# Inner products in place of halves for twelve of tile 1's outer products, with GpSimd summing and storing earlier

## The chip, the cores and the metric

The kernel runs on one core of one Trainium2 chip. The metric is the device time of one execution in microseconds (us). Before the change it is 1041.65 us, the median of three runs (1039.41 to 1042.3).

The engines are named as in the profile: PE is TensorE's matrix multiply, PEld its weight load, DVE is VectorE, ACT is ScalarE, POOL is GpSimd and SP is SyncE. A name such as ACTq is the sequencer of an engine, which also issues DMAs.

## The reference

Two blocks in a row, all in f32. First a retention layer, then a gated feed-forward layer on its output:

```
ret = (q k^T / sqrt(64)) * decay(head, row, column)     # 8 batches, 8 heads, 576 positions, 64 wide
x   = ret v, heads side by side                         # 4608 tokens x 512
g   = x @ w_gate ; h = g * sigmoid(g) * (x @ w_val)     # 4608 x 1536
out = h @ w_out                                         # 4608 x 512
```

## The kernel before

**Tiles.** The 4608 tokens are cut into tile 0 (512 tokens) and tiles 1 to 4 (1024 tokens each). Each tile has an up stage (`x @ w_gate`, `x @ w_val`) and a down stage (`h @ w_out`). The retention of later tokens is cut into ticks, whose small 64 x 64 multiplies are put between those of the stages. Tile 0 is computed plainly (`up0`, `down0`, `out0`). Tiles 1 to 4 use fast matrix multiplication, in which sums of blocks replace some multiplies.

**The up stage (`up_stage`, line 1114).** The 1536 hidden columns are cut into three quarters `qd`, each with its gate and value weights. In a quarter there are seven outer products, taken in the order `SETS = (1, 2, 6, 7, 4, 5, 3)`, one for each set of operand blocks. On the weight side, sets 1, 2, 7 and 3 are blocks of the weights as loaded, and sets 5, 6, 7 and 4 are made by outer sums (`outer_sums` in `w_sets`, two instructions of 128 x 512 each; 7 in place). The activation side has its own outer sums (`outer_sums` in `x_sets`).

An outer product is a 2 x 2 block product and is done in one of two ways:

- Plain (`PLAIN`, line 110): eight slots, two for each of its four corners. The accumulator holds a corner, which is read once or twice (`whole_read`).
- As seven inner products: seven slots. They need further, smaller sums on both sides (`inner_sums`, four sums of 128 x 256 on the activation side and four on the weight side for each set), and their banks are read in part (`first_read`), then again (`second_read`), because corners are put together from several products. The slots are numbered 1 to 7 as in `PLACE`. Slots 7 and 4 of an outer product are done among the slots of the next one.

A slot (`multiply`) is two f32 multiplies of a 128 x 128 weight block with 128 x 256 activations into one PSUM bank, four records of PE in the profile. Four banks, bankA, bankB, bankC and bankE, go round (`free`, `taken`).

Before the change all 21 outer products of tile 1 are plain, and all those of tiles 2 to 4 are inner. Tile 1 (`busy` in the code) also prepares the weights for the others: POOL makes the outer and inner sums of all 21 weight sets, and ACT's queue stores them to DRAM (`up_sets`), raw blocks in two DMAs of 256 KB and the four sums in one of 512 KB. Tiles 2 to 4 fetch them again (`fetch`, ACT's queue).

**Who does what in an up stage.** Sums from banks are DVE's (`combine`, line 1040, is the line that most of them carry), some reads are split into an ACT copy and a POOL sum. When a corner is complete, `finish` has ACT compute silu (line 1177) and, in tile 1, DVE multiply (line 1178); in tiles 2 to 4 POOL multiplies.

**The order.** Nothing is scheduled automatically: the order of the program is the order on each engine's queue. `later(at, ...)` puts work at slot `at`; `go` issues it. A down stage has 26 steps (`down_step`, line 1331) of 12 PE records each; its last five or nine steps also issue the first activation sums of the next tile (`x_first`, line 1079), two at a time, all on POOL. `down0` runs twelve steps of tile 0 in `down_order`. Between them POOL and DVE make the sums of `w_out` (`out_sums`, line 886). `out0` copies the four banks into `hid0[0]`, `[1]`, `[4]` and `[5]` and SP stores them. Those places are where sets 6, 4 and 5 of quarter 0 go next.

Of the kernel before, what the change touches and what calls it, by code (L numbers as in the profile page):

```python
# [109 lines left out]
PLAIN = {(1, qd, o) for qd in range(3) for o in SETS}  # L110
# [21 lines left out]
def kernel(  # L132
# [727 lines left out]
    down_order = [8, 9, 10, 0, 1, 11, 2, 3, 4, 5, 6, 7]  # L860
# [6 lines left out]
    def out0():  # L867
        for i, (bank, o) in enumerate(zip(banks, (hid0[f] for f in (0, 1, 4, 5)), strict=True)):
            nc.scalar.copy(out=o, in_=bank)
            nc.sync.dma_start(out=out[i * P : (i + 1) * P, :], in_=o)  # L870
# [17 lines left out]
    up_sets = [[dr.tile([P, 2048], F32, name=f"up{qd}_{o}") for o in SETS] for qd in range(NQ)]  # L888
# [91 lines left out]
    TURN = {1: [5, 6, 7, 0, 1, 2, 3, 4], 2: [7, 0, 1, 2, 3, 4, 5, 6], 3: [7, 3, 4, 5, 6, 0, 1, 2], 4: [7, 5, 6, 0, 1, 2, 3, 4]}  # L980
# [8 lines left out]
    def fetch_one():  # L989
        what, a, i, lo, width = fetches[fetched[0]]  # L990
        dst = operands[:, lo : lo + width]
        fetched[0] += 1
        if what == "dn":
            queue = nc.sync if a + 1 == NTILE and i >= 8 or a == 1 and i >= 5 else nc.scalar
            queue.dma_start(out=dst, in_=dn_ops[i])
            return
        src = up_sets[a][SETS.index(i)].rearrange("p (g x) -> p g x", g=2)
        nc.scalar.dma_start(out=dst.rearrange("p (g x) -> p g x", g=2), in_=src[:, :, P : 1024])
# [47 lines left out]
    def x_sets(n):  # L1046
# [8 lines left out]
        new = {o: spots[3 * m : 3 * m + 3] for m, o in enumerate((1, 2, 7, 4, 5, 3, 6))}  # L1055
# [23 lines left out]
    def x_first(n):  # L1079

        x_outer, x_inner, *_ = x_sets(n)
        p = nc.gpsimd
        first = x_inner(1, p) + x_outer(5, p) + x_outer(6, p)
        return first + x_outer(3, p) + x_inner(2, p) + x_outer(7, p) if n + 1 == NTILE else first

    def w_sets(qd):
# [3 lines left out]
        new = [rest[:, a : a + 1024].rearrange("p (g j x) -> p g j x", g=2, j=4) for a in (x0_at + 1024, sum_at)]  # L1090
        queue = nc.scalar
        order = (6, 4, 5, 7, 1, 2, 3)
# [5 lines left out]
        def inner_sums(o):  # L1098
            z = lambda k, m: sets[o][:, :, m, k * P : (k + 1) * P]
            to = lambda j: new[order.index(o) % 2][:, :, j]  # L1100
# [5 lines left out]
        def store(o, new_ones):  # L1106
            dst = up_sets[qd][SETS.index(o)].rearrange("p (g x) -> p g x", g=2)
            if new_ones:
                return [lambda: queue.dma_start(out=dst[:, :, 512:1024], in_=new[order.index(o) % 2].rearrange("p g j x -> p g (j x)"))]
            return [lambda m=m: queue.dma_start(out=dst[:, :, TB * (1 - m) : TB * (2 - m)], in_=sets[o][:, :, m]) for m in range(2)]  # L1110

        return sets, order, outer_sums, inner_sums, store

    def up_stage(n):
# [13 lines left out]
        number = {2: 0, 4: 1, 5: 0, 3: 1}  # L1128
# [15 lines left out]
        def to(k, c):  # L1144
            o = seq[k][1]
            return held[c] if o in (1, 6) else kept(k, c) if o == 7 else ends[number[o]][c]
# [4 lines left out]
        def weights_of(k):  # L1151
            qd, o = seq[k]
            if busy:
                sets = w_sets(qd)[0]
                spot = [(kk, m) for m in (1, 0) for kk in range(2)]
                return lambda at: sets[o][:, :, spot[at][1], spot[at][0] * P : (spot[at][0] + 1) * P]
            _, _, _, lo, width = fetches[base + k]
            w = operands[:, lo : lo + width].rearrange("p (g i x) -> p g i x", g=2, x=P)
            return lambda at: w[:, :, at if plain[k] else at - 1]
# [20 lines left out]
        def made(k, c, at):  # L1180
            if seq[k][1] in final:
                waiting.append((at + 3, k, c))

        def whole_read(k, c, bank, at):
            o = seq[k][1]
            if o == 1:
# [8 lines left out]
        def first_read(k, c, bank):  # L1195
            qd, o = seq[k]
            dst = to(k, c)
            if o == 1:
                nc.scalar.copy(out=dst, in_=bank)
            elif o == 5 and c != 12:  # L1200
# [6 lines left out]
            elif qd > 0 and o != 3 and c != 12:  # L1207
                t = ends[0 if o == 4 else 1][c]
# [64 lines left out]
        if not busy:  # L1273
            begin = lambda k: begins[k]
            if n + 1 < NTILE:
                for i, f in enumerate(x_outer(3, nc.vector)):
                    later(i, f)
                for i, f in enumerate(x_inner(2, nc.gpsimd)):
                    later(1 + i, f)
                for i, f in enumerate(x_outer(7, nc.vector)):  # L1280
                    later(3 + 2 * i, f)
# [4 lines left out]
        else:  # L1286
            for i, f in enumerate(x_outer(5, nc.vector) + x_outer(6, nc.vector) + x_outer(7, nc.vector) + x_outer(3, nc.vector)):
                later(i if i < 4 else 2 * i + 2, f)
            for qd in range(NQ):
                at = begins[len(SETS) * qd]  # L1290
                _, order, w_outer, w_inner, store = w_sets(qd)
                for i, f in enumerate([f for o in (5, 6, 7, 4) for f in w_outer(o)]):
                    later(at + i, f)
                for i, o in enumerate(order):
                    for j, f in enumerate(w_inner(o)):
                        later(at + 8 + (13 * i + 3 * j) // 2, f)
                    later(at + 8 + (13 * i + 9) // 2 + 6, *store(o, True))
                for i, o in enumerate((1, 2, 6, 7, 4, 5, 3)):
                    for j, f in enumerate(store(o, False)):
                        later(at + 3 + 5 * i + 2 * j, f)  # L1300

        def go(at):
# [9 lines left out]
            if busy and at in (120, 124, 128):  # L1312
# [15 lines left out]

    firsts = []

    def down_step(n, i):
# [37 lines left out]
        begins = N - 5 if n + 2 < NTILE else N - 9  # L1369
        if i == begins and n + 1 < NTILE:  # L1370
            firsts.extend(x_first(n + 1))
        if i >= begins:
            for f in [firsts.pop(0) for _ in range(min(2, len(firsts)))]:
                f()

# [66 lines left out]
    for m, f in enumerate(down_order):  # L1442
# [7 lines left out]
        if groups:  # L1450
            groups.pop(0)[1]()
    out0()
# [60 lines left out]
```

## Time and profile before

| what | value |
|---|---|
| median of 3 runs | 1041.65 us (1039.41 to 1042.3) |
| profiled execution, its own time | 1044.91 us |
| its span, first to last instruction | 1043.2 us |
| mean granted TensorE clock | 0.997 |
| PE / PEld busy | 98% / 80% |
| DVE / POOL / ACT busy | 66% / 53% / 28% |
| tile 0's down stage (line 864) | 123.6 to 176.6 us |
| tile 1's up stage (line 1163) | 176.6 to 338.0 us |
| tile 1's down stage (line 1342) | 338.0 to 418.0 us |
| up stages of tiles 2, 3 and 4 begin | 418, 638 and 844 us |

How to read it: a row of the timeline is a run of like instructions on one engine, with its start, its length, the engine, the line, the operation, what it writes and reads, the shape and the count; the brackets hold the idle time before it and what ended that. A PE row of eight records is two slots; its length includes the modelled end of the last record, so the pace is read from the starts of successive rows. A view by stretches gives the busy time and the count of instructions of each engine between two times.

### The profile page before, as it was taken

Reading aid. Unit: us, or ns where it says so; the run is one execution under the profiler, and the core shown is the slowest. Engines: PE = TensorE matmul, PEld = TensorE weight load, DVE = VectorE, ACT = ScalarE, POOL = GpSimd, SP = SyncE. Lnnn points to the kernel's source line nnn. Section 1 sums busy time; section 2 is a strip of 40 time slices with the busy share of each in tenths; the row PEclk is TensorE's granted clock in tenths of the full one; section 3 lists DMA queues with packets and bytes.
Section 4 is the critical chain, followed back from the end, with each engine's and each line's share of the span. In section 5 each row is a group of like instructions: output and inputs, shape, how many; then the busy total and the mean of one; then the engine's idle time right before and its main releaser. Section 6 shows DMA issues by size and latency. Waiting matters only on the chain. (4 is left out here: it accounts for less than half of the span.)

```text
span 1043.2 us, 21372 instructions
## 1 busy us (share of the span) xinstructions
PE 1018.3 (98%) x8380; PEld 834.0 (80%) x8380; DVE 692.1 (66%) x1182; ACT 288.2 (28%) x638; POOL 551.0 (53%) x586
## 2 busy tenths in 40 slices
PE   6999999999999999999999999999999999999998
PEld 5655555888788888878888887888888888888887
DVE  4488883675857855875768777857576448566744
ACT  4466532131332321123332111133230012333110
POOL 3402263884635206854657237775582497566615
PEclk9999999999999999999999999999999999999999
DMA  9999887679485886756558767544454444445552
GB/s 241 253 273 240 213 226 252 204 190 253 134 244 156 224 240 198 198 170 172 177 157 242 202 169 203 168 148 142 142 190 152 154 157 150 169 141 176 185 159 96
DMA packets 292364, 197.13 MB, mean 189 GB/s; under 512 B 212968, under 2 KB 251112, under 8 KB 292264
## 3 DMA queue, kind: packets, MB, share of 16 engines
q10 hardware_dynamic: 58960, 121.12, 35.3%
q1 hardware_dynamic: 232664, 74.25, 29.9%
q8 instruction: 66, 1.08, 0.4%
q0 software_dynamic: 640, 0.39, 0.2%
q14 instruction: 34, 0.28, 0.1%
HBM read 154.04 MB, written 41.68 MB: 188 GB/s over the span
## 5 line engine op out<-in xcount | busy, mean ns | idle before, releaser
L1041 POOL TENSOR_TENSOR rest<-rest 128x512 f32<-128x512 f32 (+1 forms) x147 | 155.6, 1073 | 158.6 <-DVE rest L1041 118.9
L1178 POOL TENSOR_TENSOR arena<-rest,io 128x256 f32<-128x256 f32 x144 | 105.4, 744 | 70.8 <-ACT io L1177 70.4
L1177 ACT ACTIVATE io<-rest 128x256 f32<-128x256 f32 x192 | 79.4, 417 | 225.1 <-DVE rest L1041 121.4
L1041 DVE TENSOR_TENSOR rest<-bankA,rest 128x512 f32<-128x512 f32 x100 | 67.7, 686 | 63.2 <-PE bankA L1163 46.2
L1163 PE MATMUL bankE<-rest,arena 128*128 128x256 f32 x424 | 108.0, 380 | 1.3 <-DVE rest L1041 1.2
L1163 PE MATMUL bankB<-rest,arena 128*128 128x256 f32 x416 | 106.4, 381 | 0.2
L1163 PE MATMUL bankA<-rest,arena 128*128 128x256 f32 x392 | 99.9, 381 | 1.4 <-DVE rest L1041 1.2
L1041 DVE TENSOR_TENSOR rest<-bankE,rest 128x512 f32<-128x512 f32 x108 | 73.0, 685 | 41.4 <-PE bankE L1163 23.8
L1041 DVE TENSOR_TENSOR rest<-bankC,rest 128x512 f32<-128x512 f32 x100 | 67.8, 685 | 44.0 <-PE bankC L1163 22.5
L1163 PE MATMUL bankC<-rest,arena 128*128 128x256 f32 x372 | 94.7, 381 | 0.6 <-DVE rest L1041 0.5
L1041 DVE TENSOR_TENSOR rest<-bankB,rest 128x512 f32<-128x512 f32 x101 | 68.7, 686 | 38.2 <-PE bankB L1163 25.0
L1163 PEld LDWEIGHTS bankE<-rest,arena 128*128 128x128 f32 x424 | 79.9, 190 | 14.1 <-DVE rest L1041 2.2
L1163 PEld LDWEIGHTS bankB<-rest,arena 128*128 128x128 f32 x416 | 78.2, 190 | 12.3 <-DVE rest L1041 1.1
L1163 PEld LDWEIGHTS bankA<-rest,arena 128*128 128x128 f32 x392 | 73.8, 190 | 13.6 <-DVE rest L1041 1.8
L1163 PEld LDWEIGHTS bankC<-rest,arena 128*128 128x128 f32 x372 | 69.8, 190 | 12.0 <-DVE rest L1041 2.5
L886 POOL TENSOR_TENSOR rest<-rest 128x256 f32<-128x256 f32 x43 | 35.4, 845 | 67.0 <-DVE rest L407 35.4
L1342 PE MATMUL bankE<-arena 128*128 128x256 f32 x264 | 61.0, 381 | 0.0
L1342 PE MATMUL bankC<-arena 128*128 128x256 f32 x264 | 60.8, 380 | 0.0
L1041 POOL TENSOR_TENSOR rest<-arena 128x256 f32<-128x256 f32 x42 | 31.5, 770 | 51.5 <-DMA up<-rest 51.5
L1342 PE MATMUL bankA<-arena 128*128 128x256 f32 x240 | 55.4, 380 | 1.8 <-POOL arena L886 1.8
L1342 PEld LDWEIGHTS bankC<-arena 128*128 128x128 f32 x264 | 50.0, 190 | 6.9
L1342 PEld LDWEIGHTS bankE<-arena 128*128 128x128 f32 x264 | 49.8, 190 | 6.9
(255 smaller groups left out, 1948.0 us busy)
## 6 DMA issues: line engine op xcount, KB each, us to landing
arena<-up ACTq DMA_DIRECT2D x63, 896.0 KB, 5.0
arena<-dn ACTq DMA_DIRECT2D x65, 384.0 KB, 4.4
arena<-dn SPq DMA_DIRECT2D x39, 384.0 KB, 3.6
up<-arena ACTq DMA_DIRECT2D x42, 256.0 KB, 4.5
up<-rest ACTq DMA_DIRECT2D x21, 512.0 KB, 3.3
dn<-rest SPq DMA_DIRECT2D x78, 128.0 KB, 1.8
out_dram<-rest SPq DMA_DIRECT2D x31, 256.0 KB, 2.6
qk<-in_q_dram SPq DMA_DIRECT2D x108, 72.0 KB, 3.2
```

The source lines that it names most:

```text
L886: eng.tensor_tensor(out=dst, in0=srcs[0], in1=srcs[1], op=ALU.add if op[0] == "add" else ALU.subtract)
L1041: eng.tensor_tensor(out=out, in0=a, in1=b, op=ALU.add if sign > 0 else ALU.subtract)
L1163: m = nc.tensor.matmul(b[:, g * TB : (g + 1) * TB], w[:, g], x, start=(opens and g == 0), stop=True, skip_group_check=True)
L1177: nc.scalar.activation(out=s, in_=src[:, 0:TB], func=AF.Silu)
L1178: (nc.vector if busy else nc.gpsimd).tensor_tensor(out=hid[:, qd, 2 * H + h, 2 * T + t], in0=src[:, TB : 2 * TB], in1=s, op=ALU.mult)
L1342: nc.tensor.matmul(b[:, m * TB : (m + 1) * TB], lhs[:, qd, ts(m, P)], w[:, qd], start=(opens and qd == 0 and m == 0), stop=(qd == NQ - 1), ...
```

## The change

It consists of these parts:

1. In tile 1, sets 6, 7, 4 and 3 of every quarter are done as seven inner products; sets 1, 2 and 5 stay plain. Twelve outer products change. The sums of the weights are read where POOL made them (`new`), in three blocks of 1024 columns instead of two.
2. The partial reads of those products: for set 6 the corner 11, for sets 7 and 4 the corners 11 and 22 go over an ACT copy and a POOL sum (`first_read`); all others are DVE's.
3. `early_sums`: in the last three steps of `down0` POOL begins the weight sums of quarter 0 (outer 5, inner 1, outer 7, inner 2, inner 7) and DVE makes tile 1's outer activation sums. To free their places, `down_order` takes hidden blocks 4 to 7 before 0 to 3, and `out0` writes to `part[8:12]`.
4. POOL issues the DMAs of the sums (`store`, 512 KB each); SP issues those of the raw blocks, and the unused 128 columns of each half are left out. A stored set is 1792 columns instead of 2048 and is fetched in one piece for each partition.
5. `x_first` gives the next tile's outer activation sums 6 and 3 (for tile 4 also 5 and 7) to DVE instead of POOL, and `up_stage` of tiles 2 and 3 loses outer sum 3 at its start.
6. Times of the other sums and of the first fetches for tile 1's down stage are set anew.

```diff
-PLAIN = {(1, qd, o) for qd in range(3) for o in SETS}
+PLAIN = {(1, qd, o) for qd in range(3) for o in (1, 2, 5)}
...
-    down_order = [8, 9, 10, 0, 1, 11, 2, 3, 4, 5, 6, 7]
+    down_order = [8, 9, 10, 4, 5, 11, 6, 7, 0, 1, 2, 3]
...
-        for i, (bank, o) in enumerate(zip(banks, (hid0[f] for f in (0, 1, 4, 5)), strict=True)):
+        for i, (bank, o) in enumerate(zip(banks, part[8:12], strict=True)):
...
-        first = x_inner(1, p) + x_outer(5, p) + x_outer(6, p)
-        return first + x_outer(3, p) + x_inner(2, p) + x_outer(7, p) if n + 1 == NTILE else first
+        p, v = nc.gpsimd, nc.vector
+        one, two = x_inner(1, p), x_inner(2, p)
+        six, three = [x_outer(o, v) for o in (6, 3)]
+        if n + 1 == NTILE:
+            five, seven = [x_outer(o, v) for o in (5, 7)]
+            rows = [[five[0], one[0]], [five[1], one[1]], [six[0], one[2]], [six[1], one[3]], [three[0]], [three[1]],
+                    [seven[0], two[0]], [seven[1], two[1]], two[2:]]
+        else:
+            rows = [x_outer(5, p), one[:2], [*one[2:], six[0]], [six[1], three[0]], [three[1]]]
+        return dict(zip(range(N - len(rows), N), rows))
...
-        new = [rest[:, a : a + 1024].rearrange("p (g j x) -> p g j x", g=2, j=4) for a in (x0_at + 1024, sum_at)]
-        queue = nc.scalar
-        order = (6, 4, 5, 7, 1, 2, 3)
+        blocks = (rest[:, x0_at + 1024 : x0_at + 2048], extra_at(1536, 1024), extra_at(0, 1024))
+        new = {o: blocks[b].rearrange("p (g j x) -> p g j x", g=2, j=4) for o, b in {6: 1, 1: 2, 7: 0, 4: 2, 2: 1, 5: 1, 3: 0}.items()}
...
             if new_ones:
-                return [lambda: queue.dma_start(out=dst[:, :, 512:1024], in_=new[order.index(o) % 2].rearrange("p g j x -> p g (j x)"))]
-            return [lambda m=m: queue.dma_start(out=dst[:, :, TB * (1 - m) : TB * (2 - m)], in_=sets[o][:, :, m]) for m in range(2)]
+                return [lambda: nc.gpsimd.dma_start(out=dst[:, 6 * P :], in_=new[o].rearrange("p g j x -> p (g j x)"))]
+            raw = dst[:, 0 : 6 * P].rearrange("p (g x) -> p g x", g=2)
+            return [lambda: nc.sync.dma_start(out=raw[:, :, P:], in_=sets[o][:, :, 0]),
+                    lambda: nc.sync.dma_start(out=raw[:, :, 0:P], in_=sets[o][:, :, 1, P:])]
...
+    def early_sums():
+        x_outer = x_sets(1)[0]
+        _, _, w_outer, w_inner, store = w_sets(0)
+        p = [w_outer(5), w_inner(1) + store(1, True), w_outer(7), w_inner(2) + store(2, True), w_inner(7) + store(7, True)]
+        v = [f for o in (5, 6, 3, 7) for f in x_outer(o, nc.vector)]
+        return p, v
...
-            elif o == 5 and c != 12:
+            elif o == 5 and c != 12 and not busy:
...
-            elif qd > 0 and o != 3 and c != 12:
-                t = ends[0 if o == 4 else 1][c]
+            elif (qd > 0 or busy) and o != 3 and c != 12 and not (busy and (o, c) == (6, 22)):
+                t = dst if busy and o == 4 else ends[0 if o == 4 else 1][c]
                 nc.scalar.copy(out=t, in_=bank)
                 combine(nc.gpsimd, dst, t, addend(k, c), 1)
...
-            for i, f in enumerate(x_outer(5, nc.vector) + x_outer(6, nc.vector) + x_outer(7, nc.vector) + x_outer(3, nc.vector)):
-                later(i if i < 4 else 2 * i + 2, f)
+            for o, at in {6: 6, 7: 12, 4: 20, 3: 33}.items():
+                for i, f in enumerate(x_inner(o, nc.gpsimd)):
+                    later(at + i, f)
             for qd in range(NQ):
                 at = begins[len(SETS) * qd]
...
+                if qd:
+                    outers = {5: 0, 6: 2, 7: 8, 4: 14}
+                    inners = {6: 4, 1: 10, 7: 14, 4: 20, 2: 29, 5: 33, 3: 37}
+                else:
+                    outers, inners = {6: 0, 4: 10}, {6: 2, 4: 16, 5: 29, 3: 37}
...
-            if busy and at in (120, 124, 128):
+            if busy and at - begins[2 * len(SETS)] in (40, 42, 45):
                 fetch_one()
...
+        if m == 9:
+            early, early_x = early_sums()
+            go_on(len(pieces))
+        if m >= 9:
+            for f in [f for fs in early[:2] for f in fs]:
+                f()
+            del early[:2]
+        if m >= 10:
+            for f in early_x[:4]:
+                f()
+            del early_x[:4]
```

## The prediction

> **What bounds the kernel now.** I read the page's first part, then the busy times by stage, then the order of work around tile 1's up stage engine by engine. The page, with busy time of each engine:
>
> ```profile
> PE 1018.3 (98%) x8380; PEld 834.0 (80%) x8380; DVE 692.1 (66%) x1182; ACT 288.2 (28%) x638; POOL 551.0 (53%) x586
> ```
>
> The stretches, from left to right: bounds, length, busy time and count of PE, PEld, DVE, ACT, POOL, clock, DMA share, GB/s. The first line is tile 1's up stage, the second tile 2's, in which all products are inner:
>
> ```profile
> 176.60:338.00 161.40, 158.87 (x1285) 138.17 (x1284) 103.72 (x181) 42.59 (x103) 97.76 (x110) 0.99 0.72 199
> 418.00:560.70 142.70, 140.04 (x1161) 119.23 (x1151) 108.43 (x190) 42.58 (x94) 89.47 (x103) 1.00 0.65 186
> ```
>
> PE is full in both. So a slot less is a slot's time less, unless another engine becomes late. The slot's time, from PE's timeline:
>
> ```profile
> 181.77 1.89 PE L1163 MATMUL bankE<-x_odd,arena 128*128 128x256 f32 x8
> 183.50 1.89 PE L1163 MATMUL bankA<-x_odd,arena 128*128 128x256 f32 x8
> ```
>
> Eight records, two slots, start 1.73 us apart: 0.8635 us a slot. Next, who has room. POOL's timeline at the border of tiles 0 and 1:
>
> ```profile
> 164.22 1.26 POOL L886 TENSOR_TENSOR rest<-rest 128x256 f32<-128x256 f32 x1 [0.54 <-DMA dn<-rest]
> 181.23 10.94 POOL L1041 TENSOR_TENSOR arena<-arena 128x512 f32<-128x512 f32 x8 [15.75 <-DMA out_dram<-arena]
> ```
>
> POOL ends tile 0's sums at 165.5 and stands still for 15.75 us, because the places of sets 5, 6 and 4 are still being stored as output. And the prices of POOL's and DVE's sums, by form (count, busy us, mean ns, idle before):
>
> ```profile
> L1041 POOL TENSOR_TENSOR arena<-arena 128x512 f32<-128x512 f32 x24 | 32.2, 1374 | 19.6 <-DMA out_dram<-arena 15.8 <-issue 3.9
> L1041 POOL TENSOR_TENSOR rest<-arena,rest 128x256 f32<-128x256 f32 x42 | 32.0, 763 | 1.6
> L1041 POOL TENSOR_TENSOR rest<-arena 128x256 f32<-128x256 f32 x42 | 31.5, 770 | 51.5 <-DMA up<-rest 51.5
> L1041 POOL TENSOR_TENSOR rest<-rest 128x512 f32<-128x512 f32 x86 | 111.0, 1299 | 157.8 <-DVE rest L1041 118.9 <-ACT rest L1209 36.5 <-ACT rest L1201 2.0
> L1041 DVE TENSOR_TENSOR rest<-bankA,rest 128x512 f32<-128x512 f32 x21 | 14.2, 685 | 26.9 <-PE bankA L1163 26.9
> ```
>
> **Part 1, the slots.** Before, 21 products of 8 slots are 168; after, 9 of 8 and 12 of 7 are 156. The built program has 24 multiplies of 128x256 less in the up stages, which is 12 slots. 12 x 0.8635 = 10.4 us off PE's path.
>
> **Part 2, is POOL in time?** The inner products need POOL's weight sums at once, where before nothing in tile 1 read them. The dangerous place is the first changed product, set 6 of quarter 0, slots 16 to 20. Tile 1 begins at 176.6, so slot 16 is due at 176.6 + 16 x 0.8635 = 190.4. Its slot 18 ends at 193.0; then DVE adds corner 11 for the second time, and must wait for POOL's first sum of that corner. Behind that wait on DVE stands the first read of corner 12, and slot 22 (the deferred slot 7 of set 6) needs it in the same bank. Slot 22 is due at 195.6.
>
> POOL's queue up to that first sum, in the built order, from 165.5 on: outer 5, inner 1 and its store, outer 7, inner 2, store, inner 7, store, outer 6, inner 6, store, inner sums of x for 6, outer 4, inner sums of x for 7, one of inner 4, then the sum. That is 8 sums of 128x512 at 1.374 (11.0), 17 weight sums of 128x256 at 0.767 (13.0), 8 sums of x at 0.753 (6.0, the row of 128x256 rest<-rest), 4 DMA issues at 0.59 (2.4) and 1.3 for the sum itself: 33.7 us, so it ends at 199.2. DVE's two reads at 0.69 follow with little overlap, and slot 22 starts near 200.5 instead of 195.6: a stall of 4.9 us. With the cheapest rows (1.27, 0.70, 0.55 for a DMA) the sum takes 31.2 us and the stall is 2.4. With every small sum at the dearest row, below, it is 12.4. I take 4.9, since the mean rows come from this same stage with DVE as busy.
>
> After that the walk shows no second late sum in quarter 0: POOL's sum for (7,11) ends at 204.9, DVE's read of it then frees its bank at 205.5, wanted at 205.8. In quarters 1 and 2 POOL has 8 x 1.374 + 28 x 0.767 + 5 x 1.3 + 7 x 0.59 = 43.1 us, and about 4 us more because set 5's sums wait in the same block for set 2's store to land. PE has 52 slots, 44.9 us, and some 5 of attention multiplies. 47 against 50 holds, with little to spare.
>
> The price of a POOL DMA issue comes from its only rows, the first two lines below; the third is ACT's 512 KB store of today (count, ns min/median/max):
>
> ```profile
> L692 POOL DMA_DIRECT2D rest<-in_v_dram x4: 585/592/601, 46.1 to 47.9; - x4
> L687 POOL DMA_DIRECT2D rest<-in_q_dram x8: 548/556/757, 33.3 to 37.3; - x8
> L1109 ACTq DMA_DIRECT2D up<-rest x21: 520/521/756, 196.3 to 342.4; - x21
> ```
>
> POOL's own issue thus holds it about as long as ACT's queue, and landing was 5.1 us for 32 KB on POOL's queue against 3.3 us for 512 KB on ACT's. The Trainium skill (DMA: Bandwidth & Descriptors, Issuing engine by pattern) sends plain stores to SP and calls that path generally faster than GpSimd's, which speaks against this part; by its fit (Anatomy of one DMA, 2.0 us and bytes over 436 thousand for each us) a 512 KB store would be an estimated 3.2 us and the 4 us above would be 3. No run here shows a 512 KB store from POOL.
>
> **Part 3, DVE and ACT.** Seven reads instead of four for a product, of which five in a quarter go over ACT and POOL: DVE gets 7 more reads a quarter, 21 x 0.685 = 14.4 us, and loses tile 1's outer sums of x from 181 on (4.7 us). 103.7 + 9.7 = 113 us of some 156 is 73%. Tile 2's stage has 108 of 142.7 and there PE stands still 1.7 us beyond the first 12 us, by the starts of its rows. At tile 1's end ACT's first fetch waits for the store of quarter 2's set 5, and silu stands behind it. For all this I add 2.0 us, near tile 2's row. The ends are 0 (reads are only added, so no gain) and 6 (tile 2's 1.7 in each quarter and one slot at the end). The eight outer sums of x now lie at 167 to 177, where DVE was idle for 16.3 us before its first read of tile 1; they cost nothing there, and 0.69 to 1.45 us each if that cover were gone.
>
> **Part 4, the tile borders.** Three stalls of PE stand at the starts of tiles 2, 3 and 4. For tile 2 DVE waits for POOL's outer sum 6, PE for DVE; for tile 4 the POOL chain delays a sum of the down stage:
>
> ```profile
> 419.31 2.88 DVE L1041 TENSOR_TENSOR rest<-rest 128x512 f32<-128x512 f32 x2 [2.34 <-POOL rest L1041]
> 427.95 1.10 PE L1163 MATMUL bankA<-rest,arena 128*128 128x256 f32 x4 [0.79 <-DVE rest L1041]
> 841.47 2.86 PE L1342 MATMUL bankA<-arena 128*128 128x256 f32 x12 [1.76 <-POOL arena L886]
> ```
>
> By the starts of successive PE rows they cost 1.6, 1.7 and 1.9 us, 5.2 in all. Sums 6 and 3 (all four for tile 4) move to DVE's idle time in the down steps: DVE is busy 4.6 us of the 13 before 418. A read that comes later would cost there, but DVE idles 1.2 to 2.0 us between two reads of a step and a sum is 0.69, or 1.44 beside POOL, so I count no loss. Gain between 0 and 5.2; I take 3.6, because POOL still makes the other half for tiles 2 and 3.
>
> **Parts at nothing.** Stores leave ACT's queue, but ACT is at 42.6 of 161 us and off the path. Raw stores go onto SP before the loads of q, k and v and wait there for POOL's outer sums, up to 194.2 for set 4; the loads lead their ticks by two ticks of 17 to 19 us (tick multiplies at 241.7, 258.7 and 277.7), and if that cover goes a tick waits by the difference. The new `down_order` takes blocks that are all ready; `out0`'s new places are first written again by set 7, from slot 21 on.
>
> **The sum.** -10.4 + 4.9 + 2.0 - 3.6 = -7.1 us. Against the profiled execution: 1044.91 - 7.1 = 1037.8, with 1.7 outside its span of 1043.2. That execution was 3.3 us above the median, so against the median 1041.65 - 7.1 = 1034.6.
>
> **Rivals.** A measurement of this kernel can tell 0.3%, 3.1 us, from no change.
>
> B, POOL is on time: 31.2 us or less up to the first sum. Then -10.4, 0 to 2.4, 0 to 2, -3.6 to -5.2: about 1029, from 1027.5 to 1031. For it: the cheap rows are POOL's when DVE is quiet. Against it: DVE has eight sums to do in the same time. 0.18.
>
> C, the borders give nothing and the reads cost 6: -10.4 + 4.9 + 6 = +0.5, or less with a part of either; 1039 to 1044. For it: the reads of four banks in strict order, DVE at 73%. 0.15.
>
> D, slower: POOL and DVE slow each other, and POOL becomes the bound of tile 1. Rows of POOL and of DVE from the same views:
>
> ```profile
> 424.91 1.06 POOL L1041 TENSOR_TENSOR arena<-arena,rest 128x256 f32<-128x256 f32 x1
> 425.93 0.73 POOL L1041 TENSOR_TENSOR rest<-rest 128x256 f32<-128x256 f32 x1
> 189.55 1.48 DVE L1178 TENSOR_TENSOR arena<-rest,io 128x256 f32<-128x256 f32 x1
> 208.78 0.42 DVE L1178 TENSOR_TENSOR arena<-rest,io 128x256 f32<-128x256 f32 x1
> ```
>
> The same shapes take 1.06 beside DVE's sums and 0.73 without, and DVE's product 1.48 beside POOL's and 0.42 alone. With all small sums at 1.06 the stall in quarter 0 is 12.4, and a later quarter has 51.3 + 4 on POOL against 51.9 with attention and waits, 3.4 late, twice: -10.4 + 12.4 + 6.8 + 2.0 - 3.6 = +7.2, 1049. It decides from a mean of about 1.0 us (+2.3). Against it: the mean was 0.767 with DVE 64% busy. 0.13. The Trainium skill (GPSIMD Engine Reference, Specifications) says that POOL shares its SBUF interfaces with DVE and that DVE instructions with two SBUF inputs contend; these rows agree, and by the rule alone every sum that meets one would be dear, which is case D.
>
> That the twelve slots would not go is excluded by the built order.
>
> **Chances.** Forecast 0.54 (1031 to 1038.5), B 0.18, C 0.15, D 0.13. Faster 0.72, the same 0.15, slower 0.13. 1027.5 to 1042.5 leaves out D, the top of C and the tail of B, about 0.19.
>
> **What would show it.** Right: slots in tile 1 at 0.8635; POOL's sums for quarter 0 from about 165.5; one PE stall of 3 to 7 us near 196 to 201, ended by DVE behind POOL; the stalls at 427, 647 and 841 gone or shorter, at earlier times. Wrong: stalls in each quarter that name POOL, small sums near 1.0 us, POOL waiting long for its own stores, or new stalls in the down stages.

## The result

The change makes the kernel slower: 1047.97 us (median of 18 runs, 1042.75 to 1054.06) against 1040.76 of the kernel before (18 runs); the ratio is 1.0063, 95% interval 1.004 to 1.0086. The forecast was 1034.6, and its range ended at 1042.5.

### The profile page after: what moved, and what is told of

The parts are those of the page before. It is cut to its first block, busy times and chain, and to the rows that moved or that the text cites. A ratio compares the mean times of both kernels' runs of the same rounds, so it can differ in the third digit from the quotient of the medians.

```text
span 1048.6 us, 21422 instructions
## 1 busy us (share of the span) xinstructions
PE 1015.3 (97%) x8332; PEld 829.5 (79%) x8332; DVE 726.8 (69%) x1216; ACT 294.5 (28%) x653; POOL 582.9 (56%) x626
## 4 chain that ended last, share of the span: by engine, by line
PE 82%; POOL 6%; DVE 5%; issue 3%; DMA 2%; ACT 1%; SPq 0%; ACTq 0%; DVEq 0%; POOLq 0%
PE bankC L1183 10%; PE bankA L1183 9%; PE bankE L1183 9%; PE bankB L1183 9%; PE bankE L1374 7%; PE bankB L1374 6%; PE bankC L1374 6%; PE bankA L1374 6%; POOL arena L1040 3%; DVE rest L1040 3%; PE bankE L853 2%; PE bankA L853 2%; PE bankC L853 2%; PE bankB L853 2%; PE inner L1183 2%
## 5 line engine op out<-in xcount | busy, mean ns | idle before, releaser
L1040 POOL TENSOR_TENSOR rest<-rest 128x512 f32<-128x512 f32 (+1 forms) x160 | 172.7, 1090 | 169.0 <-DVE rest L1040 115.1
L1183 PE MATMUL bankA<-rest,arena 128*128 128x256 f32 x428 | 111.9, 384 | 12.1 <-DVE rest L1040 12.0
L1183 PE MATMUL bankC<-rest,arena 128*128 128x256 f32 x396 | 102.7, 383 | 0.5 <-DVE rest L1040 0.3
L1183 PEld LDWEIGHTS bankA<-rest,arena 128*128 128x128 f32 x428 | 80.9, 191 | 26.2 <-DVE rest L1040 13.3
L1183 PE MATMUL bankB<-rest,arena 128*128 128x256 f32 x352 | 90.4, 381 | 0.5 <-DVE rest L1040 0.4
L1183 PEld LDWEIGHTS bankE<-rest,arena 128*128 128x128 f32 x404 | 76.7, 191 | 12.3 <-DVE rest L1040 1.9
L1183 PEld LDWEIGHTS bankC<-rest,arena 128*128 128x128 f32 x396 | 75.0, 191 | 12.7 <-DVE rest L1040 1.8
L1040 POOL TENSOR_TENSOR arena<-arena 128x256 f32<-128x256 f32 (+1 forms) x84 | 76.7, 931 | 15.0 <-PE bankA L1183 6.5
L1183 PEld LDWEIGHTS bankB<-rest,arena 128*128 128x128 f32 x352 | 66.1, 190 | 11.3 <-DVE rest L1040 2.3
L1374 PE MATMUL bankB<-arena 128*128 128x256 f32 x264 | 60.8, 380 | 0.0
L1374 PEld LDWEIGHTS bankB<-arena 128*128 128x128 f32 x264 | 50.0, 190 | 6.9
```

The source lines that it names most:

```text
L1040: eng.tensor_tensor(out=out, in0=a, in1=b, op=ALU.add if sign > 0 else ALU.subtract)
L1183: m = nc.tensor.matmul(b[:, g * TB : (g + 1) * TB], w[:, g], x, start=(opens and g == 0), stop=True, skip_group_check=True)
L1374: nc.tensor.matmul(b[:, m * TB : (m + 1) * TB], lhs[:, qd, ts(m, P)], w[:, qd], start=(opens and qd == 0 and m == 0), stop=(qd == NQ - 1), ...
```

## The profile after

The profiled execution took 1050.28 us, its span 1048.6, at a mean granted clock of 0.988 (before: 0.997). The page's first part:

```profile
PE 1015.3 (97%) x8332; PEld 829.5 (79%) x8332; DVE 726.8 (69%) x1216; ACT 294.5 (28%) x653; POOL 582.9 (56%) x626
```

PE has 48 records less, which is the twelve slots, but the shares hardly differ. The stretches show where the time went (columns as in the prediction): tile 1's up stage, tile 2's, then eight microseconds at the end of each quarter of tile 1:

```profile
178.10:351.40 173.30, 155.66 (x1238) 131.41 (x1237) 126.44 (x204) 50.50 (x120) 131.98 (x154) 0.95 0.65 178
...
431.20:571.50 140.30, 138.98 (x1135) 119.11 (x1133) 104.36 (x187) 42.24 (x94) 85.95 (x101) 1.00 0.63 184
```

```profile
226.00:234.00 8.00, 5.25 (x23) 3.69 (x22) 7.79 (x12) 1.25 (x3) 4.68 (x4) 1.00 0.49 172
274.00:282.00 8.00, 7.83 (x37) 6.55 (x35) 7.72 (x18) 4.16 (x12) 5.39 (x8) 1.00 0.52 174
338.00:346.00 8.00, 4.63 (x17) 3.03 (x15) 7.88 (x14) 2.04 (x6) 4.09 (x3) 0.88 0.93 250
```

Tile 1's up stage is 173.3 us instead of 161.4, although it has 10.4 us less to do. Tile 2's is 140.3 instead of 142.7, and the stalls at the starts of tiles 2, 3 and 4 are gone. DVE is busy 126.4 of 173.3 us, 73%; at the quarters' ends it is 97% (the time in which one of its instructions waits for POOL counts as busy).

By the starts of successive PE rows, PE stands still 19.4 us in tile 1 (waits over 0.4 us; 2.8 before): 6.4 at slot 22 of quarter 0, 3.2 at the end of quarter 0, 1.8 at 251, 3.5 between quarters 1 and 2, 4.4 at the end of quarter 2. Some 7 us more are lost because PE's rows afterwards run at half pace (17.0 us at half clock, 13.9 of them with work). Slot 22, on PE, DVE and POOL in the timeline:

```profile
203.51 2.08 PE L1183 MATMUL bankA<-rest,arena 128*128 128x256 f32 x4 [6.25 <-DVE rest L1040]
...
202.17 0.69 DVE L1040 TENSOR_TENSOR rest<-bankC,rest 128x512 f32<-128x512 f32 x1 [7.12 <-POOL rest L1040]
...
200.87 1.26 POOL L1040 TENSOR_TENSOR rest<-rest 128x512 f32<-128x512 f32 x1
```

This is the predicted stall in its predicted chain: POOL's first sum ends at 202.1, 24.0 us after tile 1 begins (predicted 22.6), DVE waits for it, PE for DVE. The row of PE, four records, takes 2.08 us instead of 1.03. The clock in the stretches around it (the third figure from the end of a line):

```profile
195.00:200.70 5.70, 2.26 (x11) 1.65 (x9) 0.04 (x1) 0.00 (x0) 5.62 (x7) 1.00 1.07 236
200.70:207.50 6.80, 3.99 (x9) 3.20 (x10) 2.67 (x4) 0.71 (x2) 6.32 (x9) 0.50 0.20 81
207.50:214.00 6.50, 6.50 (x31) 5.72 (x30) 3.46 (x5) 1.44 (x3) 4.58 (x6) 1.00 0.00 0
```

Some 3.4 us after PE fell idle the granted clock went to 0.50 and stayed there for 6.8 us, 4.0 of them after work had begun again. Half clock also follows the shorter waits at 282 to 286 (0.8 and 2.4 us idle; 3.4 us at half clock) and at 340 to 344 (1.6 and 1.8; 6.8); before the change only one such stretch lay in tile 1. The Trainium skill (TensorE: Matmul & The Clock Gate, Part 1) says that an idle window of about 3.4 us halves PE's clock and a busy one of that length restores it; this row agrees. Others fit less well: before the change 2.1 us of idle time (279.9 to 282.0) was followed by 3.4 us of half clock, while 3.4 us in e14 below (336.8 to 340.3) was followed by none. Here the measurement decides: the length alone doesn't tell.

## The experiments

Each is timed against the kernel before, side by side on the same chip: e1 to e4 in one group, e5 to e8, e9 to e12 and e13 to e16 in others, e17 alone. The median of the kernel before moved between 1040.4 and 1042.5 from group to group, so between groups the ratios are the better measure, and differences under 2 us are not read. A second measure, from the traces, is the time from the start of tile 1's up stage to the start of tile 2's, called the block here: 241.8 us before the change, 253.0 after. It leaves out what lies ahead of tile 1, which differs by up to 8 us between the profiled executions (tile 1 begins at 172.4 to 180.7 us), though of the edits from e2 on only e15's reaches that far ahead.

| run | edit | median us (runs) | ratio to before, 95% |
|---|---|---|---|
| changed kernel | | 1048.0 (18) | 1.0063 (1.004 to 1.0086) |
| e1_borders | before, part 5 of the change only | 1034.7 (12) | 0.9943 (0.9914 to 0.9972) |
| e2_six_dve | quarter 0's set 6 read by DVE alone | 1051.9 (6) | 1.0082 (1.0051 to 1.0113) |
| e3_three_split | set 3 read over ACT and POOL | 1047.8 (12) | 1.0044 (1.0019 to 1.007) |
| e4_silu_psum | silu in PSUM | 1046.4 (12) | 1.0028 (1.0007 to 1.0049) |
| e5_all_plain | all of tile 1 in eight slots | 1029.3 (4) | 0.9892 (0.9866 to 0.9918) |
| e6_set3_plain | set 3 in eight slots | 1043.4 (10) | 1.0011 (0.9989 to 1.0034) |
| e7_q0_plain | quarter 0 in eight slots | 1045.8 (10) | 1.0054 (1.0033 to 1.0074) |
| e8_fill | PE kept busy ahead of slot 22 | 1049.7 (7) | 1.006 (1.0028 to 1.0091) |
| e9_set3_psum | e6 and e4 | 1040.0 (10) | 0.997 (0.9944 to 0.9996) |
| e10_q0_set3_psum | e7, e6 and e4 | 1032.5 (6) | 0.9912 (0.9877 to 0.9948) |
| e11_plain_psum | e5 and e4 | 1032.9 (7) | 0.991 (0.9878 to 0.9943) |
| e12_q0_psum | e7 and e4 | 1039.3 (10) | 0.9969 (0.9947 to 0.9992) |
| e13_fetch_sp | first down fetches on SP's queue | 1047.2 (7) | 1.0063 (1.0039 to 1.0087) |
| e14_e10_fetch_sp | e10 and e13 | 1031.0 (4) | 0.9917 (0.9885 to 0.9949) |
| e15_store_sp | the sums' stores issued by SP | 1049.5 (5) | 1.0093 (1.0062 to 1.0123) |
| e16_q0_set3_fetch | e14 with silu back in SBUF | 1040.2 (10) | 0.9997 (0.9973 to 1.0021) |
| e17_fetch_pool | e14, those fetches on POOL's queue | 1029.9 (6) | 0.9893 (0.9867 to 0.992) |

### The borders alone

e1_borders is the kernel before with the new `x_first`, its steps in `down_step` and the two lines of `up_stage` that belong to them.

> The kernel before with part 5 alone (the next tile's outer sums 6 and 3, for tile 4 also 5 and 7, on DVE in the last down steps). If the border stalls are a gain of their own, all three stalls at the starts of tiles 2, 3 and 4 go (5.2 us by the starts of PE rows, 6.5 by the lengths of the stages) and the kernel is 5 to 6.5 us faster than before, about 1035. Rival: the stalls went in the changed kernel only because tile 1 left the queues in another state; then the time stays within 2 us of before.

1034.7 us: the borders are worth 5.9 us (2.9 to 9.0), more than the 3.6 of the sum, though the interval holds 3.6 too. The traces say the same: tile 2's up stage is 1.7 us shorter than before, tile 3's up stage 2.2 and its down stage 2.0, 6.0 in all. What is lost is lost elsewhere.

### One wait at a time

```diff
 e2_six_dve
-elif (qd > 0 or busy) and o != 3 and c != 12 and not (busy and (o, c) == (6, 22)):
+elif (qd > 0 or busy) and o != 3 and c != 12 and not (busy and (o == 6 and (qd == 0 or c == 22))):
 e3_three_split
-elif (qd > 0 or busy) and o != 3 and c != 12 and ...
+elif (qd > 0 or busy) and (o != 3 or busy) and c != 12 and ...
-    t = dst if busy and o == 4 else ...
+    t = dst if busy and o in (4, 3) else ...
 e4_silu_psum
-s = io[:, (silus[0] % 4) * TB : (silus[0] % 4 + 1) * TB]
+s = outer[:, 1, 256:512] if busy else io[:, (silus[0] % 4) * TB : (silus[0] % 4 + 1) * TB]
```

> The changed kernel, but in quarter 0 DVE itself makes the first sum of corner 11 of set 6, so nothing there waits for POOL. Theory of the late sum: the stall of 6.4 us before slot 22 and the half-clock records behind it (2.1 us) go, 8 us less than the changed kernel, about 1040. Rival, POOL is late in general: the wait moves to the sums of set 7 a few slots on, and under 3 us are won. Rival, DVE is the bound of the quarter: the time is lost again at the quarter's end, 3 to 5 us won.

1051.9 us, no gain. DVE no longer waits for the sum of (6,11), but for the next one, of (7,11); its row in e2's timeline:

```profile
202.47 0.69 DVE L1040 TENSOR_TENSOR rest<-bankB,rest 128x512 f32<-128x512 f32 x1 [7.41 <-POOL rest L1040]
```

POOL begins that sum at 201.2, 27 us after tile 1 begins; PE passes slot 22 without a wait and stands still 4.7 us some six slots later. What is late is POOL's whole queue, not one sum.

> The changed kernel, but set 3's first reads of corners 11 and 22 go over an ACT copy and a POOL sum, as those of sets 7 and 4 do: DVE loses two of the seven reads that it has at the end of each quarter. Theory of bunching (DVE's queue holds more than PE's time in the last three products of a quarter): the stalls at the quarter ends (3.2, 3.5 and 4.4 us, and 6 us of half clock behind the last two) fall by half or more, 6 to 10 us less than the changed kernel. Theory of the shared port (DVE's products wait for POOL's trains of sums): no change beyond 2 us, or longer, since POOL has more to do.

1047.8 us. The stalls at the three ends fall from 3.2, 3.5 and 4.4 us to 1.6, 2.3 and 3.5, but one of 2.6 appears at 302 where there was none, and the one at 251 grows. POOL got what DVE lost, and DVE's product waits for POOL: the two ahead of these stalls take 4.4 us (248.0) and 4.1 (296.6).

> The changed kernel, but tile 1's silu goes to PSUM (one place instead of four), so that DVE's product reads one operand from SBUF instead of two. Theory of the shared port: all 48 products of tile 1 take 0.45 us or less (now up to 4.7, mean 0.62), the stall of 1.8 us at 251 goes and those at the quarter ends shrink: 5 to 9 us less than the changed kernel. Theory of bunching: the long products go too, but the stalls at the quarter ends stay at over half, and 2 to 4 us are won.

1046.4 us. DVE's products by form in tile 1's up stage, of the changed kernel and of e4 (count, busy us, mean ns, idle before):

```profile
L1198 DVE TENSOR_TENSOR arena<-rest,io 128x256 f32<-128x256 f32 x45 | 38.8, 878 | 6.4 <-ACT io L1197 6.4
```

```profile
L1198 DVE TENSOR_TENSOR arena<-rest,outer 128x256 f32<-128x256 f32 x45 | 18.5, 411 | 13.0 <-ACT outer L1197 12.9
```

With one input in PSUM the product takes 0.41 us and none over 1; DVE has 20 us more to spare, and the stall at 251 goes. The others stay. Each of three suspects taken away alone thus gives little: e2 nothing, e3 0.2 us by the medians and 2.0 by the ratios, e4 1.6 and 3.6.

### All products plain, everything else changed

```diff
-PLAIN = {(1, qd, o) for qd in range(3) for o in (1, 2, 5)}
+PLAIN = {(1, qd, o) for qd in range(3) for o in SETS}
```

The `x_inner` sums of four sets in tile 1, which only inner products read, are left off POOL as well.

> The changed kernel with all 21 products of tile 1 in eight slots as before (the four inner sums of x, which only inner products use, are left off POOL too); early weight sums, POOL's own stores and the borders stay changed. Theory 1 (the loss comes with the inner products: seven PSUM reads for four, bunched on DVE at the quarters' ends, and PE reading POOL's sums at once): no stall over 1 us in tile 1's up stage, stage 161 to 163 us, time that of the borders alone, 1033 to 1037. Theory 2 (the loss comes from POOL's sums and stores in their new order, which hold up DVE and PE whoever reads them): stalls stay, stage over 166 us, time 1040 or more.

1029.3 us. The changed kernel is some 18 us above this one (1.71% of 1041), although it has 10.4 us less to do, so the inner products lose 28 (by the block, 253.0 against 235.9, 27.5). And e5 is 5 us below e1: the earlier sums of POOL and DVE with the new stores gain that much, and which of them does is not told apart. Theory 2 falls. e5's stretches, tile 1's up stage and the ends of quarters 1 and 2:

```profile
176.50:332.80 156.30, 156.25 (x1284) 137.18 (x1285) 110.96 (x179) 43.29 (x105) 97.94 (x121) 1.00 0.70 192
```

```profile
272.00:280.00 8.00, 8.00 (x163) 6.99 (x162) 8.00 (x14) 2.39 (x6) 4.24 (x3) 1.00 0.48 78
324.00:332.00 8.00, 8.00 (x39) 7.04 (x38) 8.00 (x16) 1.96 (x5) 1.66 (x2) 1.00 0.37 89
```

DVE is as full at the ends of quarters 1 and 2 as in the changed kernel, 8.00 of 8 us (5.8 at the end of quarter 0), and PE waits nowhere. A full DVE by itself is therefore not the cause. What differs is how late a read may be.

### Set 3, quarter 0, and PE's idle time

e6 has `(1, 2, 5, 3)` in `PLAIN` (and no `x_inner` of set 3); e7 has all sets of quarter 0 there, with the `x_inner` sums behind that quarter's products; e8 issues one multiply five times:

```diff
 e8_fill
-multiply(b, weights_of(k)(PLACE[i]), x_at(seq[k][1], i, seq[k][0]), opens)
+for _ in range(5 if busy and (k, i) == (3, 1) else 1):
+    multiply(b, weights_of(k)(PLACE[i]), x_at(seq[k][1], i, seq[k][0]), opens)
```

> The changed kernel with set 3, the last of each quarter, in eight slots too (three slots, 2.6 us, more for PE; nine reads of 0.61 to 0.69 us less for DVE, all at the quarters' ends; x sums of set 3 left off). Theory 1 (DVE bunched at the quarters' ends): the stalls at the three ends, 3.2, 3.5 and 4.4 us, fall to 1 us or less each and the half-clock stretches behind the last two go; the stall of 6.4 us at slot 22 stays; time 1039 to 1043. Rival (these waits come from silu and its product in the row, not from the number of reads): stalls stay at 2 to 4 us, time 1048 to 1051.

> The changed kernel with quarter 0 of tile 1 in eight slots (four slots, 3.5 us, more; the inner sums of x move behind quarter 0's plain products). Theory 1 (POOL is late in quarter 0 as a whole): the 6.4 us at slot 22 and the half-clock stretch behind it, 3.4 us more, go, and no other stall takes their place in the first 30 us; 1041 to 1044. Rival (the wait only moves to the next sum that needs POOL, as it did with set 6 on DVE): a stall of 4 us or more in the first 40 us, time 1048 or more.

1043.4 and 1045.8 us: e6 is about 5 us better than the changed kernel, e7 1 to 2, which is short of both expectations. In e6 PE waits not at all at the end of quarter 0, 1.7 us between quarters 1 and 2, and 1.5 and 1.6 in the last third of quarter 2; in e7 the stall at slot 22 is gone. But both show a new one that neither expectation had, at 251.7 (4.3 us) and 247.4 (3.2). e6's timeline around it, on PE, DVE and POOL:

```profile
243.60 1.03 PE L1183 MATMUL bankB<-rest,arena 128*128 128x256 f32 x4
...
251.70 1.98 PE L1183 MATMUL bankB<-rest,arena 128*128 128x256 f32 x4 [4.15 <-DVE rest L1040]
...
241.82 6.91 DVE L1198 TENSOR_TENSOR arena<-rest,io 128x256 f32<-128x256 f32 x1
...
250.97 0.68 DVE L1040 TENSOR_TENSOR rest<-bankB,rest 128x512 f32<-128x512 f32 x1
...
241.39 0.58 POOL L1116 DMA_DIRECT2D up<-arena  x1 [0.30 <-POOL arena L1040]
241.99 1.29 POOL L1040 TENSOR_TENSOR arena<-arena 128x512 f32<-128x512 f32 x1
...
247.73 0.72 POOL L1040 TENSOR_TENSOR rest<-arena,rest 128x256 f32<-128x256 f32 x1
248.74 0.58 POOL L1116 DMA_DIRECT2D up<-rest  x1 [0.30 <-POOL rest L1040]
```

DVE's product begins while POOL issues a store, and ends only when POOL has done seven sums in a row. Behind it DVE reads bankB at 250.97, over 6 us after PE filled it, and the inner product's next slot needs that bank. In e5 a product of 5.07 us cost nothing:

```profile
237.08 1.89 PE L1183 MATMUL bankE<-x_odd,arena 128*128 128x256 f32 x8
...
245.38 0.81 PE L1183 MATMUL bankE<-rest,arena 128*128 128x256 f32 x3
...
237.89 5.07 DVE L1198 TENSOR_TENSOR arena<-rest,io 128x256 f32<-128x256 f32 x1
242.89 0.68 DVE L1040 TENSOR_TENSOR rest<-bankE,rest 128x512 f32<-128x512 f32 x1
```

A plain corner's bank is wanted again after the three other corners, six slots or 5.2 us; here PE comes back to bankE at 245.38, 2 us after DVE's late read. Even a product of 6.91 us would have let that read end at about 245.4, by an estimate from these rows. An inner product's slots 1, 6, 7 and 4 add to one bank, which is read between them, and only two or three other slots, 1.7 to 2.6 us, lie between. That is the loss of slack that the sum did not have. It is read from the order of the banks and from these rows; no run changes this distance alone.

> The changed kernel; in each quarter the multiply that stands just ahead of slot 22 is issued five times over (the last one counts), which puts 4 x 0.86 = 3.5 us of idle work on PE where it stands still 6.4 us in quarter 0, and lengthens quarters 1 and 2 by 3.5 us each where PE doesn't wait. Theory (PE's idle time of 6 us is what halves the granted clock afterwards): the stall is 3 us, no half-clock stretch near 201 to 208 us, quarter 0 shorter by 3.4 us, while the time as a whole is 1048 - 3.4 + 7 = 1051 or less where the fill lies in later waits. Rival (the clock halves for another reason): the half-clock stretch stays, quarter 0 as long as before, time 1055.

1049.7 us. The wait at slot 22 is 2.3 us instead of 6.4, and the half-clock stretch is 3.4 us instead of 6.8; it did not go, as the expectation had it:

```profile
193.14 4.48 PE L1183 MATMUL bankE<-x_odd,arena 128*128 128x256 f32 x20
199.78 2.08 PE L1183 MATMUL bankA<-rest,arena 128*128 128x256 f32 x4 [2.16 <-DVE rest L1040]
```

```profile
199.50:202.90 3.40, 3.12 (x7) 2.52 (x8) 1.61 (x3) 0.00 (x0) 2.92 (x5) 0.53 0.27 108
```

Slot 22 comes 24.9 us after the stage's start instead of 25.4, so quarter 0 gained little. That idle time sets the clock's stretch is supported; the length from which it does is not settled.

### Two and three edits together

> Set 3 in eight slots (as e6_set3_plain) and tile 1's silu in PSUM, so that DVE's product has one input in SBUF (as e4_silu_psum). In e6 the stall of 4.3 us at 251.7 stood behind one product of 6.91 us beside POOL's train. Theory 1 (two costs: DVE's product held up by POOL, and DVE's bunch at the quarters' ends; each edit takes one): no product over 0.5 us, no stall over 1 us after quarter 0, only the 6.5 us at slot 22 and its half clock stay; 1043.4 - 4.3 - 3 = 1036. Rival (the products' waits only lie in time that DVE has over; the port costs nothing, as e4 by itself gained 1.6 us at most): 1042 or more.

> The three edits together: quarter 0 and set 3 in eight slots, silu in PSUM; six products (sets 6, 7 and 4 of quarters 1 and 2) stay in seven slots. Theory 1 (POOL late in quarter 0, DVE's bunch, DVE's product beside POOL; nothing else): no stall over 1 us in tile 1's up stage; e5_all_plain's time less six slots, 1029.3 - 5.2 = 1024. Rival (what is left of the inner products, their sums on ACT and POOL, still makes PE wait): stalls of 1 us and more at sets 6, 7, 4; 1029 or more.

> e5_all_plain with silu in PSUM, the control for the two above: PE never waits in e5's tile 1, though DVE's product took up to 5.07 us there. Theory 1: 1029 +- 2, no gain, since a late DVE costs nothing where a product is read once in two slots. Rival (the port holds up PE everywhere by small amounts): 1026 or less.

> Quarter 0 in eight slots and silu in PSUM, set 3 of quarters 1 and 2 in seven: eight products of seven slots. It differs from e10_q0_set3_psum by set 3 alone. Theory 1 (DVE's bunch at the quarters' ends, where set 3 is the last): stalls of 2 to 5 us at the ends of quarters 1 and 2 with half clock behind them stay; 1024 - 1.7 + 8 to 14 = 1030 to 1036. Rival (the bunch is the product's wait for POOL alone): no stall over 1 us, 1022.5.

Here the runs add up. All four have silu in PSUM and ran side by side; e11 is the control, with no inner product.

- e10 has six inner products (sets 6, 7 and 4 of quarters 1 and 2). It should be 5.2 us below e11 and is 0.4 below: 4.8 lost.
- e12 has also set 3 of quarters 1 and 2: 6.8 us above e10 where two slots, 1.7 us, are saved: 8.5 lost. Stalls of 1.7 + 1.9 and of 3.3 + 1.2 us stand at the two ends, each with 6.8 us of half clock. DVE is not full there, 6.6 and 5.7 of 8 us (below). A part of the loss may be the edit's own: silu has one place there instead of four, and just ahead of the first stall three of DVE's products wait 0.45 us each for ACT's silu (266 to 268).
- e9 has sets 6, 7 and 4 of quarter 0 in addition to e10: 7.5 above it, where 2.6 are saved: 10.1 lost. The stall at slot 22 is back with 5.7 us.

e12's stretches at the ends of quarters 1 and 2:

```profile
263.00:271.00 8.00, 6.11 (x28) 4.71 (x26) 6.64 (x14) 1.55 (x4) 6.24 (x9) 1.00 0.32 131
327.00:335.00 8.00, 4.82 (x17) 3.25 (x15) 5.68 (x12) 2.75 (x8) 1.80 (x1) 0.84 0.67 214
```

The three losses make 23.4 us (set 3 of quarter 0 is in none of them). All twelve products with silu in PSUM (e4) lose 22.7 against e11 by the ratios (1.0028 - 0.991, 12.3 us, and 10.4 not gained). The rest up to 28 us is put down to the product's wait for POOL. By the block (237.5 us in e11, 241.3 in e10, 247.5 in e12, 246.4 in e9, 251.3 in e4) the three are 9.0, 7.9 and 7.7 us, 24.6 together, and e4's loss is 24.2: the sum holds by both measures, its parts are known to some 4 us. All four are slower than theory 1 said, by 3 to 8.5 us. A part of that is in the control: e11 is slower than e5 (1032.9 against 1029.3), since silu in the bank of `outer` makes the ticks' multiplies wait 0.4 to 0.8 us each for DVE's product. The largest miss, e10's, asks for a further cause.

### What is left in e10

e10's ACT and PE at the end of the up stage:

```profile
323.16 0.35 ACTq L995 DMA_DIRECT2D arena<-dn  x1
323.56 0.39 ACT L1197 ACTIVATE outer<-rest 128x256 f32<-128x256 f32 x1 [6.26 <-POOL rest L1040]
...
328.28 2.51 PE L1183 MATMUL bankE<-rest,arena 128*128 128x256 f32 x8 [3.44 <-DVE rest L1040]
```

ACT does nothing for 6.3 us: its queue holds the first fetch of down weights, which waits for POOL's store of set 5, and four silus stand behind it. (The bracket names a POOL sum that ended at the same moment; e14 shows that it is the fetch.) The next kernels move fetches and stores; in e17, `nc.gpsimd` for i < 5:

```diff
 e13, e14, e16
-queue = nc.sync if a + 1 == NTILE and i >= 8 or a == 1 and i >= 5 else nc.scalar
+queue = nc.sync if a + 1 == NTILE and i >= 8 or a == 1 else nc.scalar
 e15
-return [lambda: nc.gpsimd.dma_start(out=dst[:, 6 * P :], ...
+return [lambda: nc.sync.dma_start(out=dst[:, 6 * P :], ...
```

> The changed kernel with tile 1's first fetches of down weights on SP's queue instead of ACT's, where the first one waits for POOL's store of set 5 with silu behind it. Theory 1 (silu late behind that fetch is a part of the stalls at the end of quarter 2): these, 1.8 + 1.9 + 0.7 us with 6.8 us at half clock behind, fall to half; 1048 - 4 = 1044. Rival (the bunch of reads on DVE alone makes them): the stalls stay, 1047 to 1049.

> e10_q0_set3_psum with the same fetches on SP's queue. Theory 1 (the stall of 3.6 us at 328 and the half clock behind it, 1.7, come from ACT's fetch): both go, 1032.5 - 5.3 = 1027.2, which is e11_plain_psum's time less the six slots. Rival (DVE's reads make it): 1031 or more.

e13: 1047.2 us, no gain: of the stalls at the end of quarter 2 the first goes, the others stay. With set 3 inner, DVE is late there anyway. e14: 1031.0 us. The up stage is 155.6 us instead of 160.6, as theory 1 said, but a new wait stands in the down stage:

```profile
340.26 2.86 PE L1374 MATMUL bankE<-arena 128*128 128x256 f32 x12 [3.43 <-DMA arena<-dn]
```

SP issues the third fetch only behind ten loads of q, k and v, at 334.8.

> e14_e10_fetch_sp with tile 1's first five fetches of down weights on POOL's queue, behind the store that they wait for and ahead of no loads. Theory 1 (the fetch alone held e10 and e14 back): no stall over 1 us at the end of the up stage or the start of the down stage; 1031 - 3.4 = 1027.5. Rival (POOL, held by the fetch's wait, brings its sums for the down stage late): a stall of 2 us or more there, 1030 or more.

1029.9 us, between the two. The end of the up stage has no wait, the start of the down stage one of 1.3 us; up stage and this wait together are 156.8 us:

```profile
172.40:329.20 156.80, 152.36 (x1262) 131.90 (x1260) 98.66 (x190) 47.65 (x114) 116.81 (x148) 1.00 0.68 187
```

Against e11 the six products now pay 3.0 of their 5.2 us by the medians, 1.8 by the ratios, 0.7 by the block (236.8 against 237.5): that they pay at all is not clear of the noise. Of what is left, 1.4 us stand at 272, where a tick's multiply waits for DVE's product, and 1.5 at 277 without a cause that the trace names. The kernel is as fast as e5, which has none of the six; both beat the kernel before and the changed one.

> The changed kernel with the sums' stores issued by SP instead of POOL. Theory 1 (POOL is late in quarter 0 by its own queue, in which each store takes 0.58 us and 0.30 ahead of it): with four stores less ahead of the sum for (6,11) the stall at slot 22 falls from 6.4 to about 2.9 us, 1048 - 3.5 = 1044.5 or less. Rival (SP, which waits for each sum in order, brings the loads of q, k and v late, and PE waits there): new stalls at the attention's multiplies, 1048 or more.

1049.5 us. Slot 22's wait falls to 3.8 us, near the 2.9 expected, so POOL's own stores are some 2.6 us of its lateness. But at the end of quarter 2, in SP's, POOL's and PE's rows:

```profile
322.33 8.89 SPq L1116 DMA_DIRECT2D up<-arena  x2
...
327.95 2.90 POOL L1040 TENSOR_TENSOR arena<-arena 128x256 f32<-128x256 f32 x4 [8.12 <-DMA up<-arena]
...
339.34 2.08 PE L1183 MATMUL bankA<-rest,arena 128*128 128x256 f32 x4 [6.21 <-DVE rest L1040]
```

SP issues set 2's store behind ten loads; POOL waits 8.1 us for it to land before it makes set 5's sums in the same place; ACT's fetch waits for set 5's store, silu for ACT, DVE for silu and PE for DVE. The rival had the place wrong: not the attention's multiplies wait, but the same end of quarter 2.

> e14_e10_fetch_sp with silu back in SBUF: quarter 0 and set 3 in eight slots, first fetches on SP's queue. Theory 1 (DVE's product beside POOL's train makes PE wait wherever an inner product needs the next read at once): single products of 4 to 7 us with stalls of 2 to 4 us behind them in quarters 1 and 2, 1030 or more. Rival (it costs nothing when the other three causes are gone; silu in PSUM even costs the 2 to 3 us by which e11 is behind e5): 1024 to 1026, the fastest of all.

1040.2 us, 9.2 above e14: with six inner products left, silu in SBUF costs 9 us by the medians, where in e5 it cost nothing. (e16's ten runs lie between 1034.3 and 1043.8 us; the profiled one took 1036.1, and its block is 6.2 us longer than e14's.) In e16's timeline a product of 6.96 us and the wait behind it:

```profile
233.97 6.96 DVE L1198 TENSOR_TENSOR arena<-rest,io 128x256 f32<-128x256 f32 x1
...
243.91 1.55 PE L1183 MATMUL bankB<-rest,arena 128*128 128x256 f32 x4 [4.01 <-DVE rest L1040]
```

## Why the prediction was wrong

**Part 3 failed.** It gave 2.0 us, with ends 0 and 6, to seven reads in place of four, and it argued from a share of the stage, DVE at 73%. The share came out at 73% by luck: DVE was busy 126.4 us for the 113 of the sum, some 20 of them in products that waited for POOL, and the stage took 173.3 for 156. And it says nothing: in e5 it is 71% (111.0 of 156.3) and PE never waits. What the sum left out is the slack of each read: six slots for a plain corner, two or three for an inner product. That is argued from the bank order; the losses themselves are measured. Set 3 at the ends of two quarters loses 8.5 us; the six products of quarters 1 and 2 lose 4.8 (9.0 by the block), of which ACT's fetch, which the part named and did not price, is 2.0 by the ratios of e10 and e17 and 4.5 by their blocks; and DVE's product behind POOL is some 3 to 5 us here, 6 to 9 in e16. That makes 18 to 20 us where 2.0 stood.

**Part 2 held in place and chain, and was too small in price.** The stall at slot 22 is 6.4 us for 4.9, inside its ends. But quarter 0's inner products lose 10.1 us (e9 against e10; 7.7 by the block), 3 to 5 more than the sum has: 1.9 of it is the half clock behind the stall, and the rest is not told apart, though e2 shows POOL late for the next sum too. POOL's 512 KB stores, for which the part had no row, landed in 3.7 us in the median (2.9 to 7.2), near its 3.3 and 3.2.

**Part 1 held**: twelve slots are gone. **Part 4 was too small**: 5.9 us for 3.6 (6.0 in the traces), above its upper end 5.2. **The parts at nothing** gain 5 us (e5 against e1); that was luck, and without it the miss would be larger. Together, -10.4 + 28 - 5.9 - 5.3 = +6.4, near the 6.6 measured (0.63%); this divides the measured change and doesn't test it, since 28, 5.9 and 5.3 are differences of the same ratios.

**Half clock** is in no part. It costs some 7 us in tile 1, and a sum of long stalls must have it.

**Rival D** gave 1049 and came true in time, not in mechanism. POOL's small sums took 0.73 to 0.78 us as before, and POOL stood idle 12.5 us waiting for DVE and ACT. It was DVE that was slowed, in its product: D quoted the very row (1.48 against 0.42) and drew its price from POOL's. Rival C named the reads of four banks in strict order, which is near what happened, and stopped at 6 us.

## What to carry to other kernels

Count for each read how many slots lie between it and the next use of its bank; a busy share, even the right one, does not tell. A change that shortens that distance turns every lateness that was free before, of a product, a fetch or a store ahead in a queue, into a stall. A stall can be paid again in PE's clock: in these traces every idle stretch of PE of 3.6 us and more from tile 1's up stage on was followed by half clock, and of those between 2.1 and 3.5 us some were and some were not. When several waits lie close together, taking away one shows little: take them all away and put them back one by one.

## What the runs showed of the hardware

A DVE instruction with two SBUF inputs beside a train of POOL sums can wait for several of them, not only for one: 6.91 us for 0.41, behind seven sums, though it had begun while POOL issued a DMA. The Trainium skill (SBUF — State Buffer, SBUF: two separate sides) describes an exclusive lock that whoever starts first holds for its one instruction. By that the product would take an estimated 1.7 us at most (one sum of 1.29 and its own 0.41); the measurement differs, and decides. With one input in PSUM the product took 0.41 us beside the same trains.
